# Inverse transform along D by even and odd parts with the forward tables reused, its last 64 spectral rows column- and row-tiled

## Chip, cores, metric

The kernel runs on one core of one Trainium2 chip. The metric is the device time of one execution in microseconds. A run is one execution; medians are quoted with the range of the runs.

## The reference, cut to what matters

Forward and backward pass of a gated mix: a spectral filter (2-D real FFT of a 2048 x 576 input, times a complex filter, inverse FFT) and a GEGLU feed-forward block (576 to 4608 to 576) are mixed by a sigmoid gate. The outputs are the result and seven gradients.

```python
def _A_ref(x, w_r, w_i):                    # spectral filter
    X = rfft2(x.astype(float32), axes=(-2, -1))          # 2048 x 289
    return irfft2(X * (w_r + 1j * w_i), s=(2048, 576)).astype(bfloat16)
def _B_ref(x, w_gate, w_up, w_down):
    return (_gelu(x @ w_gate) * (x @ w_up)) @ w_down
g = sigmoid((x * gate_w).sum(-1, keepdims=True))
out = g * _A_ref(...) + (1 - g) * _B_ref(...)
# reference(): out and its vector-Jacobian product for a given grad_out
```

So two inverse transforms are needed: one for the output and one for the gradient of x. Each maps 289 complex columns to 576 real ones in 16 blocks of 128 rows.

## The kernel before

Everything is matrix multiplication with tables of cosines and sines. A first phase of 144 steps (18 groups of 8) computes the feed-forward block; the work of the FFT is cut into units, each of which takes one slot, and a pacing function puts the slots between the steps' own work. At most one unit goes ahead of a step's matmuls and one behind them. All units from here on share **one** PSUM buffer, `pf`, of two banks, and a pool of 19 SBUF buffers. A second phase multiplies with the transposed weights.

```python
LCH = [(0, 128), (128, 128), (161, 128)]     # 289 spectral columns in three chunks, 95 rows counted twice

def at_unit(lc):                             # inverse table by transposing the forward table Dt
    def f():
        l0, ln = LCH[lc]
        tps = pf.tile([P, 2, 1024], BF16, tag="pf", name="tps")
        for c in range(2):
            for ci in range(4):
                nc.tensor.transpose(tps[:, c, ci * P:(ci + 1) * P], tb.Dt[ci][:, c, l0:l0 + ln], ident[:])
            nc.tensor.transpose(tps[:, c, 512:D], tb.Dt[4][LO, c, l0:l0 + ln], ident[LO, LO])
        o = unit([2, D], name="At")
        V.tensor_copy(o[:], tps[:, :, 0:D])
        if lc == 2:
            nc.gpsimd.memset(o[0:L2NEW, :, :], 0.0)
        LD.dma_start(scr_at[lc], o[:])
    return f

def z(i):                                    # inverse along the inner 16 of S
    def f():
        ...
        for lc, (l0, ln) in enumerate(LCH):
            o = zf[:, lc * 256:(lc + 1) * 256]
            nc.tensor.matmul(o, lhsT=Vp[:, ii, 0, l0:l0 + ln], rhs=<B 1:3, 256 columns>, start=True, stop=False)
            nc.tensor.matmul(o, lhsT=Vp[:, ii, 1, l0:l0 + ln], rhs=<B 0:2, 256 columns>, start=False, stop=True)
        zt[i] = unit([3, 2, P], name="ZT")
        nc.scalar.copy(zt[i][:].rearrange("p a c m -> p (a c m)"), zf[:, 0:768])

def d(i):                                    # inverse along D
    def f():
        ...
        for lc in range(3):
            for c in range(2):
                for h in range(2):
                    nc.tensor.matmul(yps[:, h, :288], lhsT=Z[:, lc, c, :],
                                     rhs=tb.At[lc][:, c, h * 288:(h + 1) * 288], start=(n == 0), stop=(n == 5))
                n += 1
        yo = unit([2, 288], name="yo")
        <ACT copies yps to yo, with scale>
        LD.dma_start(dv[:, i, :], ...)

fft = at + fg + [gap] * 5 + mid[:-2] + [load_At] + pa + mid[-2:] + [gap] * 2 + ia[:-4] + pb + ia[-4:] + ib
```

`fg` are the forward units (u1 and u2 in turn), `mid` the middle stage (s2 and s1 units, beginning with a prefetch), `ia` and `ib` the z and d units of the two inverses. `LD` is the queue of DMA issues on SyncE.

## Time and profile before

| | before |
|---|---|
| time, median of 3 runs | 1547.2 us (1546.21 to 1549.07) |
| span of the profiled run | 1545.3 us |
| PE busy, whole span | 96% |
| first phase ends at about | 1097 us |
| z and d units lie in | 624 to 978 us |

The page's lines stand in the prediction below. Two things to know when reading them. The busy time of a group of matmuls is the union of their pipelined spans, so the price of a matmul is the distance between the *starts* of two neighbours in the timeline. And a wait is only a cost on the engine that sets the pace, here PE.

### The profile page before, as it was taken

What the parts mean: (1) busy time and instruction counts of PE and PEld (TensorE: products, weight loads), DVE (VectorE), ACT (ScalarE), POOL (GpSimd) and SP (SyncE); (2) the same over time, 40 slices, a digit from 0 to 9 for tenths busy, and PEclk for the clock granted to TensorE, in tenths of its full rate; (3) what the DMA queues carried; (4) which work ended last, traced back from release to release, by engine and by line L of the source; (5) the groups of instructions that cost most, each with busy time, mean ns of one, the idle gap of its engine ahead of it and who ended that gap; (6) DMA issues with size and microseconds to landing.
All of it is one profiled execution on the core that took longest, in us unless ns stands there. A gap on an engine that the chain in (4) does not pass through costs nothing.

```text
span 1545.3 us, 30301 instructions
## 1 busy us (share of the span) xinstructions
PE 1483.3 (96%) x11857; PEld 1082.0 (70%) x11982; DVE 825.9 (53%) x2176; ACT 711.7 (46%) x1361; POOL 22.5 (1%) x51
## 2 busy tenths in 40 slices
PE   7778999999999999999999999999998999999998
PEld 5435666676676666777776777667876777777776
DVE  6557667788787887656555555676013221211111
ACT  5455666667666766666666666665000000000000
POOL 0000000000000000000000000000000000000000
PEclk9899999999999999999999999999999999999999
DMA  5133244355444535434434434454999887878773
GB/s 180 57 101 100 81 118 119 112 145 160 121 144 145 150 91 170 118 100 114 118 96 128 133 102 131 110 150 121 268 209 220 185 174 156 169 160 166 151 152 67
DMA packets 504175, 212.23 MB, mean 137 GB/s; under 512 B 307680, under 2 KB 497120, under 8 KB 504032
## 3 DMA queue, kind: packets, MB, share of 16 engines
q1 hardware_dynamic: 500592, 204.56, 53.3%
q0 software_dynamic: 1632, 4.72, 1.1%
q8 instruction: 93, 1.52, 0.4%
q10 hardware_dynamic: 1808, 1.02, 0.2%
q14 instruction: 50, 0.41, 0.1%
HBM read 41.77 MB, written 94.71 MB: 88 GB/s over the span
## 4 chain that ended last, share of the span: by engine, by line
PE 84%; issue 10%; DVE 2%; DMA 2%; ACT 2%; SPq 0%; POOL 0%; POOLq 0%; ACTq 0%; DVEq 0%
PE wps L407 16%; PE xy L324 16%; PE acc L906 10%; PE wps L390 9%; PE z L313 8%; PE acc L864 8%; PE pf L660 3%; PE xy L321 2%; PE wps L418 2%; PE z L317 2%; PE pf L447 1%; PE pf L644 1%; PE pf L646 1%; DMA wgu<-in_B_w_gate_dram 1%; PE fx L447 1%
## 5 line engine op out<-in xcount | busy, mean ns | idle before, releaser
L324 PE MATMUL xy<-wgu,xT 128*128 128x512 bf16 x1027 | 256.7, 382 | 14.0 <-issue 11.1
L906 PEld LDWEIGHTS <-pin 128*128 128x128 bf16 x2304 | 225.4, 98 | 56.8
L407 PEld LDWEIGHTS <-xn 128*128 128x128 bf16 x2304 | 225.1, 98 | 36.0 <-issue 0.2
L324 PEld LDWEIGHTS <-xT 128*128 128x128 bf16 x1152 | 101.3, 98 | 143.8 <-issue 42.9
L335 ACT ACTIVATE da<-z,omg 128x256 bf16<-128x256 f32 x288 | 120.8, 473 | 105.3 <-PE z L317 105.2
L339 DVE TENSOR_SCALAR s<-q 128x512 bf16<-128x512 bf16 x144 | 42.0, 292 | 218.3 <-ACT q L336 217.8
L336 ACT ACTIVATE q<-xy 128x512 bf16<-128x512 f32 x144 | 86.0, 597 | 151.6 <-PE xy L324 151.6
L864 PE MATMUL acc<-wd_all,pin 128*128 128x288 bf16 x1152 | 145.4, 288 | 6.9 <-ACT f32t L869 4.5
L390 PE MATMUL wps<-dB,A 128*128 128x288 bf16 x1152 | 149.8, 286 | 0.0
L313 PE MATMUL z<-wdT,dOT 128*128 128x256 bf16 x1152 | 140.8, 277 | 3.8 <-DVE Vt L469 3.8
L906 PE MATMUL acc<-wuT,pin 128*128 128x288 bf16 x1152 | 143.4, 286 | 0.0
L906 PE MATMUL acc<-wgT,pin 128*128 128x288 bf16 x1152 | 143.4, 286 | 0.0
L864 PEld LDWEIGHTS <-pin 128*128 128x128 bf16 x1152 | 113.3, 98 | 37.5 <-issue 5.7
L390 PEld LDWEIGHTS <-A 128*128 128x128 bf16 x1152 | 112.5, 98 | 31.5
L407 PE MATMUL wps<-dHg,xn 128*128 128x256 bf16 x1152 | 131.7, 273 | 0.0
L407 PE MATMUL wps<-dHu,xn 128*128 128x256 bf16 x1152 | 131.3, 273 | 0.0
L313 PEld LDWEIGHTS <-dOT 128*128 128x128 bf16 x1152 | 113.7, 99 | 20.4 <-issue 4.2
L916 ACT COPY f32t<-acc 128x576 f32<-128x576 f32 x16 | 10.2, 638 | 249.1 <-PE acc L906 249.1
L918 DVE SCALAR_TENSOR_TENSOR f32t<-gwf,dlog,f32t 128x576 f32<-128x576 f32 x16 | 13.1, 818 | 187.6 <-ACT f32t L916 187.6
L347 ACT ACTIVATE om<-s 128x512 bf16<-128x512 bf16 x144 | 92.1, 640 | 14.8 <-DVE s L340 14.5
L348 ACT ACTIVATE s<-s 128x512 bf16<-128x512 bf16 x144 | 90.7, 630 | 4.6
L869 ACT COPY f32t<-acc 128x576 f32<-128x576 f32 x16 | 10.2, 638 | 167.4 <-PE acc L864 158.3
(185 smaller groups left out, 1859.9 us busy)
## 6 DMA issues: line engine op xcount, KB each, us to landing
scr<-A SPq DMA_DIRECT2D x144, 128.0 KB, 1.8
scr<-dHg SPq DMA_DIRECT2D x144, 128.0 KB, 1.9
scr<-dHu SPq DMA_DIRECT2D x144, 128.0 KB, 1.9
out_dram<-dw SPq DMA_DIRECT2D x67, 128.0 KB, 1.9
wd_all<-in_B_w_down_dram SPq DMA_DIRECT2D x3, 1728.0 KB, 14.2
out_dram<-dwd SPq DMA_DIRECT2D x34, 144.0 KB, 1.9
scr_p<-Vt SPq DMA_DIRECT2D x32, 144.5 KB, 2.3
Vp<-scr_p SPq DMA_DIRECT2D x16, 289.0 KB, 3.1
```

The lines of the kernel that those rows point to most:

```text
L313: nc.tensor.matmul(zt[0][:, t % 2, (t - t0) // 2, :], lhsT=dOT[:, ci, t, :], rhs=wdT[:, ci, :], start=(t < t0 + 2 and ci == 0), stop=False)
L324: nc.tensor.matmul(xy[:, tt, :], lhsT=xT[:, ci, t0 + tt, :], rhs=wgu[:, ci, :], start=False, stop=(ci == 3))
L335: nc.scalar.activation(da[:, tt, :], da_ps[:, tt, :], ACT.Copy, scale=omg32[:, t0 + tt:t0 + tt + 1])
L336: nc.scalar.activation(q[:], hg, ACT.Square)
L339: V.tensor_scalar(s[:], q[:], A_GELU, 1.0, op0=ALU.mult, op1=ALU.add)
L347: nc.scalar.activation(om[:], s[:], ACT.Sigmoid, scale=-2.0 * C_GELU)
L348: nc.scalar.activation(s[:], s[:], ACT.Sigmoid, scale=2.0 * C_GELU)
L390: nc.tensor.matmul(wps[:, :288], lhsT=tl(0, t)[:, fch * P:(fch + 1) * P], rhs=dB[:, t, h * 288:(h + 1) * 288], start=(t == 0), stop=(t == ...
L407: nc.tensor.matmul(wps[:, cc, :], lhsT=xn[:, t, (c0 + cc) * P:(c0 + cc + 1) * P], rhs=tl(k, t), start=(t == 0), stop=(t == T - 1))
L660: nc.tensor.matmul(yps[:, h, :288], lhsT=Z[:, lc, c, :], rhs=tb.At[lc][:, c, h * 288:(h + 1) * 288], start=(n == 0), stop=(n == 5))
L864: nc.tensor.matmul(bps[:, h, :288], lhsT=At[:, r, :], rhs=wd_all[:, fc, h * 288:(h + 1) * 288], start=(fc == 0), stop=(fc == NFC - 1))
L906: nc.tensor.matmul(xps[:, h, :288], lhsT=src[:, r, :], rhs=wT[:, h * 288:(h + 1) * 288], start=(k == 1 and f0 + r == 0), stop=(k == 2 and ...
```

## The change

Intent: the table of the inverse along D is symmetric, so the rows 0 to 288 of the forward table serve as inverse table. With E = the cosine part and O = the sine part of a block, y[d] = E[d] + O[d] and y[576 - d] = E[d] - O[d]: only 289 instead of 576 columns need be multiplied. The last 64 spectral rows are packed: in z two 64-column results side by side (column-tiled), in d two 64-row products one above the other (row-tiled). The table transposes go away.

```diff
-    tb.At = []
-    def at_unit(lc): ... (30 transposes in three units, three loads)
+    def tail_table():
+        nc.gpsimd.memset(tb.At2[:], 0.0)
+        for c in range(2):
+            LD.dma_start(tb.At2[64 * c + L2NEW:64 * c + 64, :], tb.Dt[2][0:DF - 256, c, :])
 ...  z(i):
-                for lc, (l0, ln) in enumerate(LCH):        # 6 matmuls of 256 columns
+                for lc in range(2):                        # 4 matmuls of 256 columns
...
+                for v in range(2):
+                    for c, r in enumerate((LO, HI)):       # 2 column-tiled pairs of 128 columns
+                        nc.tensor.matmul(zf[r, 512:640], lhsT=Vp[:, ii, v, L2:DF], rhs=tb.B[:, 1 - v + c, :],
+                                         start=(v == 0), stop=(v == 1))
+                nc.scalar.copy(zt[i][:].rearrange("p a m -> p (a m)"), zf[:, 0:640])
 ...  d(i):
-                <12 matmuls of 288 columns, one ACT copy of 576>
+                for c in range(2):
+                    for lc in range(2):                    # 4 matmuls of 289 columns
+                        nc.tensor.matmul(yps[:, c, :DF], lhsT=Z[:, 2 * lc + c, :], rhs=tb.Dt[lc][:, c, :],
+                                         start=(lc == 0), stop=False)
+                for c, r in enumerate((LO, HI)):           # 1 row-tiled pair
+                    nc.tensor.matmul(yps[:, c, :DF], lhsT=Z[r, 4, :], rhs=tb.At2[r, :], start=False, stop=True)
+                nc.scalar.activation(ev[:], yps[:, 0, :DF], ACT.Copy, scale=scale)
+                V.scalar_tensor_tensor(yo[:, 0:DF], yps[:, 1, :DF], scale, ev[:], op0=ALU.mult, op1=ALU.add)
+                V.scalar_tensor_tensor(yo[:, D - 1:DF - 1:-1], yps[:, 1, 1:DF - 1], -scale, ev[:, 1:DF - 1],
+                                       op0=ALU.mult, op1=ALU.add)
 ...
-    fft = at + fg + [gap] * 5 + mid[:-2] + [load_At] + pa + ...
+    fft = fg + [gap] * 5 + mid[:-2] + pa + ...
```

The buffer with the first two `Dt` chunks must now live until the end, where before no table buffer was held through the middle stage.

More of the change, by code (lines that the diff above doesn't have):

```diff
@@ L40 @@
 LO, HI = slice(0, 64), slice(64, 128)
+L2 = DF - 64
+L2NEW = 256 - L2
 class Unit:
@@ L197 @@
     scr_x = dram.tile([T, P, 2, DF], BF16, name="scr_x")
-    scr_at = dram.tile([3, P, 2, D], BF16, name="scr_at")
     scr_g = dram.tile([T, P, 2, DF], BF16, name="scr_g")
@@ L263 @@
     tb.Rt = []
+    tb.At2 = res.tile([P, DF], BF16, name="At2")
     hctr = [0]
@@ L474, in fwd_units @@
         return [u1(t) for t in range(T)], [u2(t) for t in range(T)]
-    tb.At = []
-    def at_unit(lc):
-        def f():
-            l0, ln = LCH[lc]
-            tps = pf.tile([P, 2, 1024], BF16, tag="pf", name="tps")
-            for c in range(2):
-                for ci in range(4):
-                    nc.tensor.transpose(tps[:, c, ci * P:(ci + 1) * P], tb.Dt[ci][:, c, l0:l0 + ln], ident[:])
-                nc.tensor.transpose(tps[:, c, 512:D], tb.Dt[4][LO, c, l0:l0 + ln], ident[LO, LO])
-            o = unit([2, D], name="At")
-            V.tensor_copy(o[:], tps[:, :, 0:D])
-            if lc == 2:
-                nc.gpsimd.memset(o[0:L2NEW, :, :], 0.0)
-            LD.dma_start(scr_at[lc], o[:])
-        return f
-    def load_At():
-        for lc in range(3):
-            o = unit([2, D], name="At")
-            LD.dma_start(o[:], scr_at[lc])
-            tb.At.append(o)
-    load_At.noslot = True
+    def tail_table():
+        nc.gpsimd.memset(tb.At2[:], 0.0)
+        for c in range(2):
+            LD.dma_start(tb.At2[64 * c + L2NEW:64 * c + 64, :], tb.Dt[2][0:DF - 256, c, :])
     def zipped(u1, u2):
@@ L641, in f @@
                 zf = zps[:].rearrange("p a b -> p (a b)")
-                for lc, (l0, ln) in enumerate(LCH):
+                for lc in range(2):
                     o = zf[:, lc * 256:(lc + 1) * 256]
-                    nc.tensor.matmul(o, lhsT=Vp[:, ii, 0, l0:l0 + ln], rhs=tb.B[:, 1:3, :].rearrange("q v m -> q (v m)"),
-                                     start=True, stop=False)
-                    nc.tensor.matmul(o, lhsT=Vp[:, ii, 1, l0:l0 + ln], rhs=tb.B[:, 0:2, :].rearrange("q v m -> q (v m)"),
-                                     start=False, stop=True)
-                zt[i] = unit([3, 2, P], name="ZT")
-                nc.scalar.copy(zt[i][:].rearrange("p a c m -> p (a c m)"), zf[:, 0:768])
+                    for v in range(2):
+                        nc.tensor.matmul(o, lhsT=Vp[:, ii, v, lc * P:(lc + 1) * P],
+                                         rhs=tb.B[:, 1 - v:3 - v, :].rearrange("q v m -> q (v m)"), start=(v == 0), stop=(v == 1))
+                for v in range(2):
+                    for c, r in enumerate((LO, HI)):
+                        nc.tensor.matmul(zf[r, 512:640], lhsT=Vp[:, ii, v, L2:DF], rhs=tb.B[:, 1 - v + c, :],
+                                         start=(v == 0), stop=(v == 1))
+                zt[i] = unit([5, P], name="ZT")
+                nc.scalar.copy(zt[i][:].rearrange("p a m -> p (a m)"), zf[:, 0:640])
             return f
@@ L655, in f @@
                 yps = pftile()
-                n = 0
-                for lc in range(3):
-                    for c in range(2):
-                        for h in range(2):
-                            nc.tensor.matmul(yps[:, h, :288], lhsT=Z[:, lc, c, :],
-                                             rhs=tb.At[lc][:, c, h * 288:(h + 1) * 288], start=(n == 0), stop=(n == 5))
-                        n += 1
-                yo = unit([2, 288], name="yo")
-                if scale is None:
-                    nc.scalar.copy(yo[:], yps[:, :, :288])
-                else:
-                    nc.scalar.activation(yo[:], yps[:, :, :288], ACT.Copy, scale=scale)
-                LD.dma_start(dv[:, i, :], yo[:].rearrange("p h d -> p (h d)"))
+                for c in range(2):
[4 more added lines that the diff above has]
+                    nc.tensor.matmul(yps[:, c, :DF], lhsT=Z[r, 4, :], rhs=tb.At2[r, :], start=False, stop=True)
+                ev = unit([DF], F32, name="ev")
+                yo = unit([D], name="yo")
+                nc.scalar.activation(ev[:], yps[:, 0, :DF], ACT.Copy, scale=scale)
+                V.scalar_tensor_tensor(yo[:, 0:DF], yps[:, 1, :DF], scale, ev[:], op0=ALU.mult, op1=ALU.add)
+                V.scalar_tensor_tensor(yo[:, D - 1:DF - 1:-1], yps[:, 1, 1:DF - 1], -scale, ev[:, 1:DF - 1],
+                                       op0=ALU.mult, op1=ALU.add)
+                LD.dma_start(dv[:, i, :], yo[:])
             return f
@@ L699 @@
     run_late(tb)
+    tail_table()
     gate()
@@ L704 @@
     ia, pa = inv_units(scr_p1, a_dv, SD2)
-    ib, pb = inv_units(scr_p2, dxa_dv, None)
-    at = [at_unit(lc) for lc in range(3)]
+    ib, pb = inv_units(scr_p2, dxa_dv, 1.0)
     mid = mid_units()
-    fft = at + fg + [gap] * 5 + mid[:-2] + [load_At] + pa + mid[-2:] + [gap] * 2 + ia[:-4] + pb + ia[-4:] + ib
+    fft = fg + [gap] * 5 + mid[:-2] + pa + mid[-2:] + [gap] * 2 + ia[:-4] + pb + ia[-4:] + ib
     fft_pos = [0]
```

## The prediction

> **What bounds the kernel now.** I read four views in this order: the 40 slices of the page, the busy time by stretch, the groups of instructions by form, and the timeline of TensorE around the units that the change touches.
>
> The slices first. The feed-forward part with the FFT work woven in ends at about 1097 us; after that comes the second phase, which the change doesn't touch.
>
> ```profile
> PE   7778999999999999999999999999998999999998
> ...
> ACT  5455666667666766666666666665000000000000
> ```
>
> TensorE is at nine tenths or more from slice 5 on. Now the stretches: columns are the stretch, its length, then busy us and instructions of PE, PEld, DVE, ACT, POOL, then granted clock, DMA share and GB/s. The inverse transforms (z and d units, 32 of each) lie in 624 to 978.
>
> ```profile
> 62.00:96.00 34.00, 25.88 (x165) 14.52 (x167) 19.77 (x52) 17.27 (x33) 1.05 (x1) 0.90 0.37 112
> ...
> 624.00:800.00 176.00, 172.99 (x1382) 125.14 (x1404) 104.94 (x289) 112.55 (x214) 0.00 (x0) 1.00 0.39 113
> 800.00:978.00 178.00, 174.89 (x1403) 127.43 (x1424) 107.30 (x295) 113.54 (x216) 0.00 (x0) 1.00 0.41 116
> ```
>
> In the inverse stage PE is busy 347.9 of 354 us (98%), DVE 60%, ACT 64%, clock full. So TensorE sets the pace there, and what counts is the time from the start of a unit's first matmul to the start of the next unit's first. In the first of these stretches (where the three table units are) PE is busy only 76%.
>
> The groups give the instructions of the inverse and of its evacuation:
>
> ```profile
> L660 PE MATMUL pf<-At,ZT 128*128 128x288 bf16 x384 | 52.3, 286 | 0.0
> ...
> L649 ACT CAST ZT<-pf 128x768 bf16<-128x768 f32 x32 | 26.0, 813 | 5.2 <-PE pf L646 4.7
> L644 PE MATMUL pf<-Btab,Vp 128*128 128x256 bf16 x96 | 22.7, 273 | 0.0
> L646 PE MATMUL pf<-Btab,Vp 128*128 128x256 bf16 x96 | 22.7, 273 | 0.0
> ```
>
> The mean of 286 or 273 ns is a latency: matmuls overlap. The cost is in the starts, which the timeline gives (start, length, line, count):
>
> ```profile
> 641.98 1.63 PE L660 MATMUL pf<-At,ZT 128*128 128x288 bf16 x12
> 643.45 1.91 PE L313 MATMUL z<-wdT,dOT 128*128 128x256 bf16 x16
> 645.29 0.39 PE L317 MATMUL z<-wdT,dOT 64*128 64x256 bf16 x4
> ```
>
> A d unit: 643.45 - 641.98 = 1.47 us for 12 matmuls, 0.1225 us each. L313: 1.84 us for 16, of which sixteen steps of 0.109 (as the L644/L646 starts show: 639.36, 639.47, ... 640.02, six in 0.66) would be 1.74. The missing 0.10 is the step from the full array to the row-tiled L317. Next, a forward unit, which has the row-tiled form that the new d will have, and a column-tiled unit, which has the form of the new z:
>
> ```profile
> 223.49 1.15 PE L447 MATMUL pf<-Dt,dOT 128*128 128x289 bf16 x8
> 224.57 0.30 PE L450 MATMUL pf<-Dt,dOT 64*128 64x289 bf16 x2
> 224.80 0.61 PE L407 MATMUL wps<-dHg,xn 128*128 128x256 bf16 x4
> ```
>
> ```profile
> 606.84 0.29 PE L606 MATMUL pf<-n,Rt 128*128 128x289 bf16 x1
> 607.06 0.30 PE L418 MATMUL wps<-dHg,xn 128*64 128x256 bf16 x1
> 607.06 0.30 PE L418 MATMUL wps<-dHu,xn 128*64 128x256 bf16 x1
> 607.19 0.27 PE L418 MATMUL wps<-dHg,xn 128*64 128x256 bf16 x1
> ...
> 608.72 0.27 PE L418 MATMUL wps<-dHu,xn 128*64 128x256 bf16 x1
> 608.93 0.30 PE L603 MATMUL pf<-n,Rt 128*128 128x289 bf16 x1
> ```
>
> Both tiled pairs start together, so a pair costs what one full matmul costs. But entering costs 0.22 instead of 0.12 (606.84 to 607.06), the first pair 0.13 instead of 0.11, and leaving 0.21 instead of 0.11 (608.72 to 608.93; and 0.23 for the L450 pair to L407). **A change of tiling costs about 0.10 us each way.**
>
> **What the Trainium skill says.** "TensorEngine Tiling (Array Packing)", Tiling Modes, Key Properties: changing the tiling mode drains TensorE. The trace agrees: 0.10 us per change. The same page, Restrictions: column tiling disables Fast Weight Load; no trace here shows what a 64-column load costs when the matmul behind it is shorter than 256 columns, which the new z has. "TensorE: Matmul & The Clock Gate", Back-to-back issue gap, gives N / 2.4 + 2.5 ns when warm: 122.5 ns for 288 columns, 109 for 256, as measured. "VectorE: DVE Perf Modes", Why PSUM operands drop a tier: float32 read from PSUM runs at the 1x rate; the trace has a float32 scalar-tensor-tensor of 128x289 from SBUF at 519 ns, which I take for the new DVE instructions.
>
> **The change part by part.**
>
> *d unit.* Out: 12 matmuls, 1.47 us. In: four full ones of 289 columns and one row-tiled pair. Three steps of 0.123, then 0.22 into the pair and 0.23 out of it: 0.82 us. Saved 0.65 x 32 = **20.8 us**. By streamed columns alone it would have been 12 x 288 against 5 x 289, 0.84 us per unit; the two changes of tiling take 0.2 back.
>
> *z unit.* Out: six matmuls of 256 columns, 0.66 us. In: four of these, then two column-tiled pairs of 128 columns: 3 x 0.109 + 0.205 into the pairs; first pair to second 0.08 (between the 0.055 that 128 columns stream in and the 0.107 seen at L418, which would be the case if the load sets it; I choose the middle); out 0.155. Sum 0.77. **Lost 0.11 x 32 = 3.4 us**: 256 columns saved are worth 0.107, and two changes of tiling cost 0.2.
>
> *Neighbours.* In the trace 9 of 32 z units and 7 of 32 d units are followed directly by the row-tiled L321, and 3 d by L418: a change of tiling that was paid already. At 0.08 to 0.10 each, **1.5 us back**.
>
> *Table units.* 30 transposes in three slots go (0.9 us of PE each, plus 3.4 us in which PE waited for DVE's copy), with six DMAs. In their place a memset and two small DMAs in the head. The slots early on, where PE is not the bound, are filled with forward units, which leave the full stage later: about two u2 (0.5 us) and a u1 (1.3 us): **2.5 us**.
>
> *ACT and DVE.* ACT's z copy shrinks from 768 to 640 columns (813 to some 700 ns), its d copy from 576 to 289 (645 to some 390): 12 us less in all, beside PE's work, worth nothing. DVE gets two instructions per d, about 0.5 us each, 32 us in the stage: from 60% to 69%, not a bound.
>
> *The buffer of the units.* There is one pf buffer. Before, one ACT copy of 0.65 us freed it; now ACT (0.39) and then two DVE instructions in a row (1.0), behind what DVE has queued. Ten of the 31 gaps from a d's last matmul to the next unit are only 2.1 to 2.3 us. Example: the d at 632.24 is evacuated from 633.91 because ACT still reads xy; with the new chain and DVE busy until 634.64, pf is free at about 635.6, while a next unit 2.1 us behind it would come at 635.2. I put **3 us of new waits** (0.3 each).
>
> Sum: -20.8 + 3.4 - 1.5 - 2.5 + 3 = -18.4 us. 1547.2 - 18.4 = 1528.8, so **1529 us**, 1.2% less.
>
> **Rivals.**
>
> *Columns decide.* If changes of tiling were hidden, d would save 0.86 and z 0.11 per unit, 31 us with the tables 33: 1514 us, just over 2%. Against it: the 0.10 us shows at every change of tiling in the trace, also in the middle of dense work.
>
> *The evacuation becomes the bound.* If every d waited about 1 us for pf, because DVE is in-order and the pair stands behind the eight GELU instructions (3.2 us a step), or these behind it, 20 to 30 us would be lost: 1545 to 1555. For it: a single buffer, three dependent instructions on two engines. Against it: 21 of the 31 gaps are 4.2 us or more, and DVE waits for q 111 us in 600 to 980.
>
> *Gain hidden elsewhere.* If PE then waits for ACT's reading of xy, part of the gain goes. Before, PE waited 2.5 us for that in the whole run, and ACT gets lighter. Little.
>
> **Range and chances.** The d saving is read from forms that the trace has, so it is sure to 2 us; z to 2 us; pf waits from 0 to 8 us; tables 0 to 5. Range 1521 to 1538. For 2% faster it has to fall below 1516.3, which asks for all terms at their best and hidden changes of tiling: 0.05. For 2% slower, over 1578: 0.01.
>
> **What would show it.** In the changed trace a d should take 0.82 us from its first matmul to the next unit's, and a z 0.77: z slower than before is the step I'd most like to see tested. PE should keep 97% or more in the inverse stage, which should be some 16 us shorter; DVE should have 64 scalar-tensor-tensor of about 0.5 us, the wait of PE for pf (released by DVE) 2 to 6 us. The second phase, from 1097 on, should have the same length. It would be wrong if the reversed write or PSUM made the DVE pair much longer than 1 us, if column-tiled loads took longer than a 256-column matmul, or if the longer-held table changed waits for SBUF buffers in the middle stage.

## The result, and the profile after

After: 1531.2 us, the median of 4 runs (1527.9 to 1532.0); before in the same rounds 1547.9. The ratio is 0.9889, 95% interval 0.9871 to 0.9907: 1.1% less, within 2%.

First the busy time by stretch, which answers to the stretches before (PE, PEld, DVE, ACT, POOL, then clock, DMA share, GB/s):

```profile
624.00:800.00 176.00, 171.34 (x1375) 116.16 (x1398) 119.99 (x332) 111.47 (x224) 0.00 (x0) 1.00 0.41 116
800.00:978.00 178.00, 172.94 (x1386) 117.71 (x1409) 122.53 (x339) 112.21 (x226) 0.00 (x0) 1.00 0.45 122
```

PE is busy 97% here (344.3 of 354 us), but this trace lacks 124 of PE's 11824 matmul records; the control's trace (c0 below), which has all of them, gives 350.2 us, 99%. The trace before lacks 125, so the prediction's 98% is a little low too. DVE has gone from 60% to 69%. Then the groups of the changed units by form:

```profile
L636 ACT CAST ZT<-pf 128x640 bf16<-128x640 f32 x32 | 22.6, 706 | 11.3 <-PE pf L633 11.0
L645 PE MATMUL pf<-Dt,ZT 128*128 128x289 bf16 x128 | 21.1, 287 | 0.0
...
L652 DVE SCALAR_TENSOR_TENSOR yo<-pf,ev 128x289 bf16<-128x289 f32 x32 | 14.5, 454 | 0.0
L653 DVE SCALAR_TENSOR_TENSOR yo<-pf,ev 128x287 bf16<-128x287 f32 x32 | 14.3, 448 | 0.0
L651 ACT ACTIVATE ev<-pf 128x289 f32<-128x289 f32 x32 | 13.7, 429 | 4.5 <-PE pf L648 3.8
```

The reversed write of L653 costs no more per element than the forward one of L652. Now the two units in the timeline of PE, first a z and then a d, each with the instruction behind it:

```profile
631.51 0.60 PE L629 MATMUL pf<-Btab,Vp 128*128 128x256 bf16 x4
632.04 0.30 PE L633 MATMUL pf<-Btab,Vp 128*64 128x128 bf16 x4
632.27 0.94 PE L409 MATMUL wps<-dHg,xn 128*128 128x256 bf16 x7
```

```profile
661.32 0.66 PE L645 MATMUL pf<-Dt,ZT 128*128 128x289 bf16 x4
661.91 0.30 PE L648 MATMUL pf<-At,ZT 64*128 64x289 bf16 x2
662.14 0.30 PE L420 MATMUL wps<-dHg,xn 128*64 128x256 bf16 x1
```

A z takes 0.76 us from its first start to its neighbour's (0.77 in the median of all), against 0.66 before; a d 0.82 against 1.47. The z unit streams 256 columns less and got **slower**.

For the rest I cut both traces at the start of each group of eight steps (its first row-tiled xy matmul, L321 before, L323 after):

| stretch | before us | after us | difference |
|---|---|---|---|
| before group 0 | 64.7 | 65.3 | +0.6 |
| groups 0 to 2 (tables, forward units) | 178.5 | 167.8 | -10.7 |
| groups 3 and 4 (middle stage begins) | 104.7 | 114.6 | **+9.9** |
| groups 5 to 9 (middle stage) | 269.3 | 267.7 | -1.6 |
| groups 10 to 15 (z and d units) | 361.3 | 347.1 | **-14.2** |
| groups 16 and 17, to the last step | 89.9 | 89.9 | 0.0 |
| second phase | 476.9 | 477.8 | +0.9 |

The inverse stage gained 14.2 us. The head gained 10.7, which I had not foreseen, and the beginning of the middle stage lost nearly all of that again, which I had not foreseen either. The waits of the changed kernel from 225 to 350 us show what was lost (who waited, for whom, us in total, times, longest):

```profile
PE pf L520 <- DMA Vp<-scr_x: 3.8, 1, 3.8
...
ACT Vt L592 <- DMA out_dram<-o: 2.7, 1, 2.7
PE pf L587 <- ACT Vt L592: 2.6, 1, 2.6
```

Two pauses of PE, neither of which the kernel before has. The first in the timeline of PE, and the queue of DMA issues ahead of it:

```profile
258.41 0.33 PE L520 MATMUL pf<-Vp,Btab 128*128 128x289 bf16 x1 [3.79 <-DMA Vp<-scr_x]
...
259.26 3.21 PE L315 MATMUL z<-wdT,dOT 128*128 128x256 bf16 x16
262.41 0.39 PE L319 MATMUL z<-wdT,dOT 64*128 64x256 bf16 x4
```

```profile
247.07 0.44 SPq L216 DMA_DIRECT2D wgu<-in_B_w_gate_dram  x1
...
254.71 0.53 SPq L221 DMA_DIRECT2D wdT<-wdT  x1
255.29 0.59 SPq L493 DMA_DIRECT2D Vp<-scr_x  x1
```

The first load of the middle stage was issued behind the weights of the next group, whose nine issues took the queue from 247.1 to 255.2 us; it landed 3.1 us later (the median of these loads). Behind the pause, sixteen matmuls of L315 take 3.15 us (259.26 to 262.41) where they took 1.84 before: the Trainium skill's "TensorE: Matmul & The Clock Gate", Part 1, says that the clock falls to half after an idle window of about 3.4 us, and a pause of 3.79 us did that here.

### The profile page after: what moved, and what is told of

It reads as the page before. It is cut to its first block, busy times and chain, and to the rows that moved or that the text cites. A ratio compares the mean times of both kernels' runs of the same rounds, so it can differ in the third digit from the quotient of the medians.

```text
span 1530.2 us, 30042 instructions
## 1 busy us (share of the span) xinstructions
PE 1462.9 (96%) x11700; PEld 1052.8 (69%) x11824; DVE 845.8 (55%) x2237; ACT 699.4 (46%) x1361; POOL 21.8 (1%) x51
## 4 chain that ended last, share of the span: by engine, by line
PE 66%; issue 24%; ACT 4%; DVE 3%; POOL 1%; SPq 1%; DMA 1%; POOLq 0%; DVEq 0%; ACTq 0%
PE wps L409 16%; PE xy L326 15%; PE z L315 8%; PE wps L392 8%; PE acc L851 3%; PE xy L323 2%; PE wps L420 2%; PE acc L893 2%; PE z L319 1%; PE pf L629 1%; PE fx L449 1%; PE pf L449 1%; PE pf L645 1%; ACT q L338 1%; ACT xb L339 1%
## 5 line engine op out<-in xcount | busy, mean ns | idle before, releaser
L893 PEld LDWEIGHTS <-pin 128*128 128x128 bf16 x2304 | 225.4, 98 | 56.8
L315 PE MATMUL z<-wdT,dOT 128*128 128x256 bf16 x1152 | 142.4, 278 | 3.5 <-DVE Vt L471 3.5
L392 PEld LDWEIGHTS <-A 128*128 128x128 bf16 x1152 | 111.3, 98 | 32.9
L315 PEld LDWEIGHTS <-dOT 128*128 128x128 bf16 x1152 | 113.4, 100 | 22.1 <-issue 3.8
L903 ACT COPY f32t<-acc 128x576 f32<-128x576 f32 x16 | 10.2, 639 | 249.1 <-PE acc L893 249.1
L349 ACT ACTIVATE om<-s 128x512 bf16<-128x512 bf16 x144 | 92.4, 642 | 15.4 <-DVE s L342 14.7
L340 ACT CAST hu<-xy 128x512 bf16<-128x512 f32 x144 | 86.9, 603 | 0.0
```

What stands on the lines that cost most here:

```text
L315: nc.tensor.matmul(zt[0][:, t % 2, (t - t0) // 2, :], lhsT=dOT[:, ci, t, :], rhs=wdT[:, ci, :], start=(t < t0 + 2 and ci == 0), stop=False)
L340: nc.scalar.copy(hu[:], hu_ps)
L349: nc.scalar.activation(om[:], s[:], ACT.Sigmoid, scale=-2.0 * C_GELU)
L392: nc.tensor.matmul(wps[:, :288], lhsT=tl(0, t)[:, fch * P:(fch + 1) * P], rhs=dB[:, t, h * 288:(h + 1) * 288], start=(t == 0), stop=(t == ...
L893: nc.tensor.matmul(xps[:, h, :288], lhsT=src[:, r, :], rhs=wT[:, h * 288:(h + 1) * 288], start=(k == 1 and f0 + r == 0), stop=(k == 2 and ...
```

## The experiments

All kernels gave correct results. The kernel before: its medians were 1549.1, 1549.0 and 1549.0 us. What I compare against is the changed kernel run again as a control (e4 to e7 ran later on the same chip, e8 on another chip), and the stretches of the traces. Groups 5 to 9 agree to 0.1 us (267.7 us in six kernels). Two other stretches vary more without being touched: groups 0 to 2 took 165.6 to 167.8 us in these six kernels, and the second phase 476.6 to 480.6. So a total is known less well than a stage.

### Control: the changed kernel again (c0_after)

No edit.

> The changed kernel again, unaltered, as the control of this chip and to see whether its two new pauses in the middle stage (3.8 us before the first s2 unit at 254.6 us, 2.6 us before an s1 unit at 314.6 us) come back. If they belong to the program, both stand at the same units, 3 to 4.5 and 2 to 3 us long, and groups 3 and 4 of the feed-forward part take about 114 us together; if they were a chance of that one execution, they are gone, these groups take about 105 us and the kernel about 1521 us. Theory: they come back; 1531 us, ratio to before 0.989.

Measured: 1532.2 us (1531.8 to 1533.0), ratio 0.9897. Both pauses are back at the same units, 4.2 us at 254.1 and 2.7 us at 314.3; groups 3 and 4 took 114.9 us, groups 10 to 15 347.1. They belong to the program.

### The last chunk untiled (e1_full_array)

```diff
-                for lc in range(2):                       # z: 4 full + 2 column-tiled pairs
+                for lc, (l0, ln) in enumerate(LCH):       # z: 6 full, 256 columns each
-                for c, r in enumerate((LO, HI)):          # d: 4 full + 1 row-tiled pair
-                    nc.tensor.matmul(yps[:, c, :DF], lhsT=Z[r, 4, :], rhs=tb.At2[r, :], ...)
+                    for lc in range(3):                   # d: 6 full, 289 columns each
+                        tab = tb.Dt[lc] if lc < 2 else tb.At2   # At2: 128 rows, the first 95 zero
```

> The even and odd form kept, but the last chunk untiled: six full matmuls of 256 columns in z, six of 289 in d, with a masked 128-row table. It streams 256 + 289 columns more per pair of units than the changed kernel. Theory (a change of tiling costs 0.1 us each way): z 0.66 and d 0.74 us instead of 0.76 and 0.82, so 0.18 x 32 = 5.8 us less, of which 1.5 to 2 us go again where a tiled neighbour had paid for the change of tiling: 3 to 5 us faster than the changed kernel. Rival (streamed columns decide): 0.23 x 32 = 7 us slower.

Measured: 1526.4 us (1524.5 to 1528.5), **5.8 us faster** than the control, whose range it doesn't touch; groups 10 to 15 took 343.5 instead of 347.1 us. In its timeline a z:

```profile
630.39 0.82 PE L629 MATMUL pf<-Btab,Vp 128*128 128x256 bf16 x6
631.04 3.66 PE L409 MATMUL wps<-dHg,xn 128*128 128x256 bf16 x32
```

0.65 us against 0.76. A d takes 0.74 (636.69 to 637.43) against 0.82. More streamed columns, less time: the rival that counted columns alone expected 7 us more and is out. The stage shows 3.6 us, within the 3 to 5 that the price of two changes of tiling per unit gives; the rest of the 5.8 lies mostly in the second phase, which the edit doesn't touch.

### ACT alone empties PSUM (e2_act_evac)

```diff
-                nc.scalar.activation(ev[:], yps[:, 0, :DF], ACT.Copy, scale=scale)
-                V.scalar_tensor_tensor(yo[:, 0:DF], yps[:, 1, :DF], scale, ev[:], ...)
+                nc.scalar.activation(ev[:], yps[:, :, :DF], ACT.Copy, scale=scale)      # both halves to SBUF
+                V.scalar_tensor_tensor(yo[:, 0:DF], ev[:, 1, :], 1.0, ev[:, 0, :], ...)  # and the reversed one alike
```

> The changed kernel, but one ACT instruction copies both halves of the d result out of PSUM, and both DVE instructions read SBUF, so the pf buffer is free after ACT. Theory (the longer chain on pf costs waits): the PE waits for DVE at the first matmul of z, 3.8 us on the matmuls in the inverse stage, go; the kernel is 3 to 5 us faster. Rival (these waits are filled otherwise or the DVE load itself is what costs): no more than 1 us of difference, or slower as ACT gets 0.23 us more per d.

First what the changed kernel's PE waited for in 600 to 980 us at the first matmul of a z:

```profile
PEld L629 <- DVE yo L653: 3.4, 5, 1.1
...
PE pf L629 <- ACT s L350: 2.0, 5, 0.5
PE pf L629 <- DVE yo L653: 1.7, 5, 0.6
```

Measured: 1527.6 us (1525.4 to 1528.3), **4.7 us faster** than the control; groups 10 to 15 took 341.8 us, 5.3 less. All waits of PE at that matmul are gone. The first stretch reads, in the control and then here:

```profile
624.00:800.00 176.00, 174.18 (x1400) 116.11 (x1397) 120.01 (x332) 111.36 (x224) 0.00 (x0) 1.00 0.42 116
624.00:800.00 176.00, 176.00 (x1417) 117.84 (x1416) 123.17 (x339) 115.63 (x226) 0.00 (x0) 1.00 0.41 116
```

PE is now busy in all of it. DVE's instructions take the same time from SBUF (460 ns) as from PSUM (454), and DVE is as loaded as before, so it was not DVE's load that cost, but the single buffer held through three instructions on two engines.

### The first prefetch three slots earlier (e3_prefetch_earlier)

```diff
-    fft = fg + [gap] * 5 + mid[:-2] + pa + ...
+    fft = fg + [gap] * 2 + mid[:1] + [gap] * 3 + mid[1:-2] + pa + ...
```

> The changed kernel with the first prefetch of the middle stage issued three slots earlier; nothing else moves. Theory (the prefetch landed late because it stood in the DMA issue queue behind the weights of the next group, since the stage now starts three slots earlier): the 3.8 us pause before the first s2 unit is gone, and with it the half clock after it (about 2 us): 5 to 6 us faster, 1525 to 1526 us. Rival (the pause comes of the smaller pool of buffers, or another wait takes its place): within 1.5 us of the changed kernel.

Measured: 1527.9 us (1526.3 to 1530.8), **4.3 us faster** than the control by the medians; groups 3 and 4 took 111.3 us, 3.3 to 3.6 less. The load is issued at 230.5 us instead of 255.3, and the pause near 254 us is gone. The other pause stays, 3.3 us. That is less than the 5 to 6 us expected. The second pause is 0.6 us longer than in the control, and now it has slow matmuls behind it:

```profile
312.11 3.46 PE L315 MATMUL z<-wdT,dOT 128*128 128x256 bf16 x16
315.50 0.46 PE L319 MATMUL z<-wdT,dOT 64*128 64x256 bf16 x4
```

Sixteen matmuls take 3.39 us, where the control took 1.84 at this place: the half clock has not gone, it has moved to the other pause. (At 3.27 us this pause is a little shorter than the window that the page named above gives; the control's 2.7 us had no such effect.) The ranges of the two kernels nearly touch, so the size is known less well than the cause.

### One buffer more in the pool (e4_unit20)

```diff
-NUNIT = 19
+NUNIT = 20
```

> The changed kernel with 20 instead of 19 buffers in the pool that the FFT units share. Theory (the even and odd form holds one table buffer through the middle stage where the kernel before held none, so an evacuation there waits until a buffer is stored to memory): the 2.6 to 3.7 us pause before an s1 unit near 314 us, released by ACT behind a DMA of o, is gone, the 3.8 us pause near 254 us stays, the kernel is 2 to 4 us faster, 1528 to 1530 us. Rival (that pause comes of the DMA queue alone, as the other does): it stays, and the kernel is the same within 1 us.

Measured: 1528.2 us (1525.8 to 1529.1), 4.0 us faster than the control; groups 3 and 4 took 111.8 us, 3.1 less. The pause near 314 us is gone, that near 254 stays (3.8 us). So an evacuation waited there for a buffer whose contents were still to be stored. In the changed kernel's queue that store of o was issued at 313.0 us, behind a group's weights, whose issues began at 306.1. The next run shows that both must come together.

### The three table units put back (e5_tables_back)

```diff
-    fft = fg + ...
+    fft = [at_unit(lc) for lc in range(3)] + fg + ...     # as before the change; their result is not used
```

> The changed kernel with the three table units (30 transposes, three copies, a memset, three stores) put back at their old place, their result unused. Forecast of the prediction: 2.5 us slower. What the stages of the two traces say instead: groups 0 to 2 go back from 167.8 to about 178 us (10 us lost) and the pause near 254 us, which came of the three slots by which the middle stage moved, goes away with the half clock after it (5 to 6 us won back); the pause of the buffer pool stays. So 2 to 6 us slower in all, 1534 to 1537 us. If groups 0 to 2 stay near 168 us, the head gain is not of the tables.

Measured: 1532.1 us (1529.9 to 1535.7), **no slower than the control** by the medians. Groups 0 to 2 took 178.3 us, as in the kernel before; groups 3 and 4 104.9, without either pause, although the pool still has 19 buffers and holds one more table; groups 10 to 15 347.4. I had expected the pause of the pool to stay, and a total 2 to 6 us higher: that was wrong. So the removal of the table units, taken alone, was worth nothing here that these runs can tell (they spread over 5.9 us, the control's over 1.2): against the control's trace, putting them back cost 10.7 us in the head and 1.6 in groups 5 to 9, and won 10.0 where the middle stage begins, because the whole list of units moved (the remaining 2.2 are of the second phase).

### One empty slot ahead of the forward units (e7_one_gap)

```diff
-    fft = fg + ...
+    fft = [gap] + fg + ...
```

> The changed kernel with one empty slot ahead of the forward units: no work for any engine, but u1 and u2 units change places in the half-steps, as they lay before. Theory (most of the head gain is not the tables' work but this parity: three slots fewer put the u2 units, which DVE evacuates, ahead of the step's xy matmuls instead of behind them): the five waits of 2.46 us of PE for DVE's Vt come back, group 0 takes 62 to 65 us instead of 57, groups 0 to 2 174 to 178. Rival (the head gain is the work of the table units): group 0 within 1.5 us of 57. The total also moves with the pause near 254 us, so the stages decide.

What PE waited for in `pf` from 80 to 129 us, first in the kernel before, then in the changed one, then in this one:

```profile
PE pf L447 <- DVE Vt L469: 12.3, 5, 2.5
```

```profile
PE pf L449 <- DVE Vt L471: 5.7, 3, 2.7
PE pf L465 <- ACT Y L457: 5.7, 6, 1.1
```

```profile
PE pf L449 <- DVE Vt L471: 14.7, 6, 2.5
```

Measured: 1549.0 us (1545.8 to 1549.4), **16.8 us slower** than the control, for a slot in which no engine does anything. The profiled run is the fastest of six; four of the six took 3 us more, of which there is no trace. The waits of 2.5 us for DVE's copy of a u2 result are back, six of them; group 0 took 61.3 us against 56.8 in the control (62 to 65 expected) and groups 0 to 2 173.5 against 167.6 (174 to 178 expected), so the place of the units does cost time, a little less than I said. How it does so is shown only in part. The waits above add up to 14.7 us here, to 11.4 in the changed kernel and to 12.3 before: what PE no longer waits for DVE it waits for ACT in part. By the clock records of the traces, group 0 also ran at half clock for 14.7 us before, 8.6 in the control and 10.2 here; in e2, with the control's own list of units, it ran so for only 3.4 us and was 2.0 us shorter. No run separates the clock from the waits. Of the 12.8 us by which its trace is longer than the control's, 5.9 lie in groups 0 to 2 and 5.3 in groups 3 and 4, where two pauses stand: 5.6 us near 284 us, again at a load of V that was issued too late (at 286.9, this time behind stores of the step and not behind weights), and 4.4 near 322.

### The empty slot in the kernel before (e8_before_gap)

```diff
-    fft = at + fg + ...
+    fft = at + [gap] + fg + ...
```

> The kernel before the change, with one empty slot put between its table units and its forward units: nothing of the change, only the place of u1 and u2 in the half-steps. Theory (the head gain is the place, not the tables' work): the five waits of 2.46 us of PE for DVE's Vt are gone or shortened to about 1.5, groups 0 to 2 take 170 to 174 us instead of 178.5, against a slot more to do later; if no pause in the middle comes of it the kernel is 4 to 8 us faster than before, 1540 to 1545 us. Rival (the tables' own work in the head is what counts): groups 0 to 2 as before or longer, the kernel 1548 to 1551 us.

```profile
PE pf L463 <- ACT Y L455: 5.1, 5, 1.3
PE pf L447 <- DVE Vt L469: 4.2, 2, 2.7
```

Measured: 1545.4 us (1544.1 to 1547.9), ratio 0.9983, interval 0.9967 to 1.0: 3.5 us faster by the medians, at the edge of what these runs can tell. The stretches are clear: groups 0 to 2 took 172.0 us against 178.5, with the waits of the lines above instead of five of 2.5 us. That lies between the theory and its rival: with the tables still there, the place alone gives 6.5 of the 10.7 us. Groups 3 and 4 took 109.6 against 104.7, with a pause of 3.2 us at a late load of V. The kernel before could have had more than half of the head gain, and would have paid for it in the same place.

### All that these runs point to (e6_all)

The edits of e1, e2, e3 and e4 in one kernel. To make room for the twentieth buffer an index table of 512 bytes per partition, used only in the head, moved into the pool.

> All that the first runs point to, together: last chunk untiled, ACT alone empties the pf buffer, first prefetch three slots earlier, 20 pool buffers (a small index table moved into the pool to make room). If the gains add: 5.8 + 4.7 + 4.3 + 3 = 18 us faster than the changed kernel, 1513 to 1516 us; groups 10 to 15 about 339 us. If they overlap (the same idle time counted twice), 1517 to 1522 us.

Measured: 1513.6 us (1513.0 to 1514.4), ratio to before 0.9776, interval 0.9761 to 0.9791: **2.2% faster than before** and 18.7 us faster than the changed kernel. The gains of the four runs, 5.8 + 4.7 + 4.3 + 4.0 = 18.8, add up in the medians. By stage, groups 10 to 15 took 337.9 us, 9.2 less than in the control (e1 and e2 alone: 3.6 and 5.3), and groups 3 and 4 106.2, 8.7 less (e3 and e4 alone: 3.6 and 3.1; the half clock that e3 only moved is gone here). No pause of PE over 0.3 us is left between 225 and 1060 us, and PE is busy in the whole inverse stage:

```profile
624.00:800.00 176.00, 176.00 (x1398) 123.97 (x1396) 124.36 (x343) 119.81 (x230) 0.00 (x0) 1.00 0.43 120
800.00:978.00 178.00, 178.00 (x1410) 124.76 (x1408) 127.04 (x350) 119.47 (x231) 0.00 (x0) 1.00 0.50 131
```

## Why the prediction was right, point by point

1. **The price of a d unit** was right: 0.82 us predicted and measured, 0.65 x 32 = 20.8 us saved.
2. **z slower than before** was right: 0.77 predicted, 0.766 the median measured, 0.11 x 32 = 3.5 us lost. The one number I had to choose, the step from the first column-tiled pair to the second (0.08 us), measured 0.078. e1 confirms the reason: without tiling both units are shorter.
3. **Neighbours**: right in kind. In the trace after, 9 z and 5 d units are followed by the row-tiled L323 and 4 d by the column-tiled L420. A z ahead of L323 takes 0.152 us from its last start to that matmul; the untiled z of e1 0.205. The size was too low: the prediction missed that L418 follows 3 z units, and from start to start, neighbours included, the 32 d units took 25.8 us instead of 48.0 and the z units 24.3 instead of 22.1. Against points 1 and 2 alone that is 1.4 and 1.3 us better, so neighbours gave 2.7 us, not 1.5.
4. **The buffer of the units** was right in mechanism and set too low: 3 us predicted, 4.7 (times) to 5.3 (stage) measured by e2. The term that was mis-sized is the wait per gap. Added up from start to start in groups 10 to 15, d gave -22.2 us, z +2.2, and all other matmuls with the waits before them +5.8: the -14.2 measured, where the prediction had some 16. Of the 5.8, e2 took 5.3 away.
5. **The table units** are the step that failed. I took their work out of the sum (2.5 us) and did not see that the whole list of units moves. Their removal was worth nothing in the total (e5), as the balance of effects that I had not named. Groups 0 to 2 show two gains: they took 178.5 us with the tables and u2 behind a step's matmuls (before), 172.0 with the tables and u2 ahead (e8), 173.5 without the tables and u2 behind (e7), 167.6 without them and u2 ahead (control). So the place is worth 5.9 to 6.5 us and the table units themselves 4.4 to 5.0. Against this, the same shift made a load and a store stand behind the weights in the one issue queue (e3 and e4), most of the 9.9 us lost in groups 3 and 4: with both mended, e6 is 8.7 us shorter there than the control. The prediction's last sentence named changed waits for SBUF buffers in the middle stage as a way to be wrong; that happened, but was paid for by the head.
6. **ACT and DVE, second phase**: right. DVE 69% as estimated; its two instructions took 454 and 448 ns against the 500 assumed (519 in the instruction they were taken from); ACT's new d copy took 429 instead of some 390; the second phase has the same length to 0.9 us.

So the inverse stage was met because its mechanism was right, but that the total of 1529 was met to about 2 us is luck in part: the head's gain of 10.7 us and the loss of 9.9 behind it, neither foreseen, happened to cancel. The rival "columns decide" was shown wrong by e1. The rival "the evacuation becomes the bound" was right in kind, at a quarter of the size that it was given. Two things are open. One is how much of the gain by place is waiting and how much the clock. The other is why the pool's pause needs just this arrangement of slots: I showed that one buffer more, or another arrangement, takes it away, not which store had to meet which evacuation in general.

## What to carry to other kernels

Count changes of tiling as matmuls: here each cost 0.096 us, nearly a 256-column matmul, so packing two 64-row pieces pays only where it removes clearly more than two matmuls per visit; a masked full-array chunk was shorter. When a change shortens a list of interleaved work, the order of everything behind it moves; look at what then stands behind what in each in-order queue. Look also at how long a single PSUM buffer is held: three instructions on two engines instead of one copy cost 5.3 us here. Compare stretches, not totals: an edit that was worth nothing in the total hid a gain of 10.7 us and a loss of 9.9.

## What the Trainium skill lacked or had wrong

- "TensorEngine Tiling (Array Packing)", Key Properties, says that a change of mode drains TensorE, but gives no price. Here it was 0.09 to 0.10 us each way at full clock (row-tiled and column-tiled alike): starts 0.202 apart instead of 0.109 into the z pairs, 0.220 instead of 0.123 into the d pair. A table of speedups without it misleads for short visits.
- The same page, Restrictions, says that column tiling disables Fast Weight Load. It doesn't say what that costs. Here a 64-column load took 107 to 110 ns where a 128 x 128 one took 98, and the two 128-column pairs of a z started 0.078 us apart, where the second pair and a column-tiled L420 behind it started 0.052 apart: at most 0.026 us per z, if the loads are the reason, which no run shows.
- "Vector Engine (DVE) Microarchitecture Reference" lists among what it didn't measure how the engine streams an operand with a negative step. A reversed bf16 output of 287 elements took 448 ns, a forward one of 289 454 ns.
- "DMA: Bandwidth & Descriptors", Issuing engines are not separate DMA queues, says that issuing from several engines only saves the sequencer's time, "which is usually small relative to the DMA itself". Here it was not small: nine issues of a group's weights held the queue for 8.2 us (247.07 to 255.29) ahead of a load that lands in 3.1, and PE paused 3.8 us for it. No run issued loads from a second engine.
